# The product with w_in by Strassen's algorithm over halves of 768 tokens, with the weight parts kept in DRAM

## The chip, the core and the metric

The kernel runs on one core of a Trainium2 chip. The metric is the device time of one execution in microseconds. Engines are named as the profile names them: PE is TensorE with its matrix multiplications, PEld its weight loads, DVE is VectorE, ACT is ScalarE, POOL is GpSimd, SP is SyncE, which here only issues DMAs.

## What is computed

```
scores = q @ k.T / 8                     # 8 x 8 heads, 576 positions, head size 64
cum    = cumsum(log(clip(f, 1e-4, 1)))   # decay along the sequence
attn   = softmax(where(causal, scores + cum_i - cum_j, -1e9))
x      = attn @ v                        # laid out as 4608 tokens x 512
h      = x @ w_in                        # w_in: 512 x 2048
g      = h * erf(softplus(h))
out    = g @ w_out                       # w_out: 2048 x 512
```

Everything is float32. w_in and w_out come to the chip as 64-bit numbers, and the kernel makes float32 of them by integer operations (`convert`).

## The kernel before

Each float32 operand of the two large products is held as two float32r parts, a rounded `h` part and the rest `l`, and a product is the sum of h*h, h*l and l*h: three matmuls.

The program has an attention part and then the part called `Moe`. The order of the instructions on PE, ACT, DVE and POOL is the order of the program; the order of the DMAs on SP is chosen when the kernel is built.

**Attention.** A loop over t, 64 + 5 steps, is a pipeline. In step t, PE makes the scores of head half-pair t, the transposes of t-3 (L423) and the products with v of t-4 (L450). DVE adds the decay (L389), ACT takes the exponentials (L401), and POOL normalises t-2 (L411), which the transposes of the next step read. Finished heads go to `xt_d` in DRAM, x transposed. At the end of each step one piece of the weight conversion is run: the first half of the weights, 16 quarters of four pieces each. Quarter u of weight tile a is half of w_in's (i < 2) or of w_out's part (i >= 2). Piece 0 is an Abs on ACT (L293), piece 1 a DVE operation that waits for it (L297), piece 2 two DVE operations (L302, L304), piece 3 a DVE operation (L307), a cast to the h part (L310), the l part on POOL (L311), and the load of the next quarter. The parts stay in SBUF.

**Moe.** Tokens are in chunks of 512, features in groups of 128. A unit is one group of features for one chunk, 144 units in all. The first five chunks are visited for the first eight feature groups, then again for the other eight (their partial sums wait in `part_d`), and the remaining four chunks for all sixteen. For each unit:

- `up` (L135): 4 pieces of the contraction x 3 = 12 matmuls of 512 columns into one PSUM bank of four;
- `softplus` from PSUM (L140) and, for three units together, `erf` (L143), each with its table load on ACT;
- `gate` on DVE (L149, L151) and the l part `gl` on POOL (L152);
- `down` (L171 to L173): 4 token blocks x 3 = 12 matmuls of 512 columns, summed in PSUM over all feature groups of a visit, and at its end copied (L201) or added to the partial sum (L199).

The x of a chunk comes by two DMAs (`xr`) and is split by ACT (L122) and POOL (L123). The first four `up` are run in steps NH to NH+3 of the attention loop, where NH = 64. The second half of the weights is converted in the loop over units, two pieces after each step:

```python
    while moe.more():
        moe.step()
        for _ in range(2):
            if todo:
                convert(*todo.pop(0))
```

## Time and profile before

| | |
|---|---|
| three runs | 1147.81, 1149.36, 1149.46 us; median 1149.36 |
| profiled execution | 1149.86 us, span 1148.1 us, mean granted TensorE clock 0.987 |
| PE busy | 1117.4 us of the span, 7264 matmuls |
| DVE, ACT, POOL busy | 564.8, 624.4, 460.8 us |
| DMA | 120.05 MB, mean 105 GB/s |

Lines of groups read: line of the kernel, engine, operation, what is written from what, shapes and count, then busy time in us and mean ns of one, then the idle time of the engine just before them and what ended it. In lines of a timeline and of the chain in order of time, the first number is the start in us from the start of the span and the second the length. In lines of windows stand the stretch, its length, the busy time of PE, PEld, DVE, ACT and POOL with the number of instructions, the granted clock, the busy share of the DMA engines and GB/s. A busy PE isn't PE at its peak, since the records of matmuls overlap: the pace is read from their starts.

### The profile page before, as it was taken

To read this page: it belongs to the slowest core of one execution; us is meant where nothing else is said; L and a number is where in the kernel's file an instruction comes from. 1 tells how busy PE (TensorE), PEld (TensorE's weight loads), DVE (VectorE), ACT (ScalarE), POOL (GpSimd) and SP (SyncE) were. 2 spreads that over 40 slices of the span, in tenths; PEclk is the share of its full clock that TensorE was granted. 3 is DMA by queue.
4 is the path that set the end of the run, shared out by engine and by line. 5 is a ranking of instruction groups with operands and counts; after the bars stand their busy time and mean duration, and the time that the engine had idled before them with its cause. 6 is when DMAs were issued, how large, how long until landed. Compare 5 with 4: busy or idle time off the path is not lost.

```text
span 1148.1 us, 19397 instructions
## 1 busy us (share of the span) xinstructions
PE 1117.4 (97%) x7264; PEld 923.5 (80%) x7264; DVE 564.8 (49%) x1475; ACT 624.4 (54%) x1251; POOL 460.8 (40%) x532
## 2 busy tenths in 40 slices
PE   5999999999989999999999999999999999999998
PEld 3888888888877878787888888888888888888886
DVE  4788888888855566666322332332322312322221
ACT  3787878787876657557442444343333343344342
POOL 1555556565563444443432432432232232233221
PEclk7999999999999999999999999999999999999999
DMA  7577778778632132230230320320000100000101
GB/s 257 169 249 255 249 231 253 237 245 236 217 118 77 56 113 86 95 109 20 74 106 5 110 98 13 110 92 19 37 19 19 37 19 19 37 19 1 37 1 37
DMA packets 57726, 120.05 MB, mean 105 GB/s; under 512 B 4768, under 2 KB 20128, under 8 KB 57632
## 3 DMA queue, kind: packets, MB, share of 16 engines
q1 hardware_dynamic: 57632, 118.80, 32.0%
q8 instruction: 58, 0.95, 0.3%
q14 instruction: 36, 0.29, 0.1%
HBM read 94.52 MB, written 24.26 MB: 103 GB/s over the span
## 4 chain that ended last, share of the span: by engine, by line
PE 89%; ACT 3%; DVE 2%; DMA 2%; POOL 1%; issue 1%; SPq 0%; ACTq 0%; POOLq 0%; DVEq 0%
PE ph L135 32%; PE y L173 10%; PE y L172 10%; PE y L171 10%; PE s L366 9%; PE o L450 8%; PE t L423 8%; PE s L371 2%; DMA wraw<-in_w_in_dram 1%; POOL xl L123 1%; DMA xr<-xt_d 1%; ACT L143 0%; ACT xh L122 0%; ACT e L143 0%; ACT L293 0%
## 5 line engine op out<-in xcount | busy, mean ns | idle before, releaser
L135 PE MATMUL ph<-xh,w 128*128 128x512 f32 x1152 | 381.7, 392 | 7.3 <-DVE e L149 7.3
L152 POOL TENSOR_TENSOR gl<-e,gh 128x512 fp32r<-128x512 f32 x144 | 186.9, 1299 | 409.0 <-DVE gh L151 392.6
L140 ACT ACTIVATE e<-ph 128x512 f32<-128x512 f32 x144 | 86.1, 598 | 372.9 <-PE ph L135 368.7
L135 PEld LDWEIGHTS ph<-xh,w 128*128 128x128 f32 x1152 | 217.9, 189 | 55.8 <-DVE e L149 7.1
L149 DVE TENSOR_TENSOR e<-e,ph 128x512 f32<-128x512 f32 x144 | 98.1, 681 | 323.6 <-ACT e L143 323.6
L135 PE MATMUL ph<-xl,w 128*128 128x512 f32 x576 | 225.5, 391 | 0.0
L172 PE MATMUL y<-w,gh 128*128 128x512 f32 x576 | 224.1, 389 | 0.0
L173 PE MATMUL y<-w,gl 128*128 128x512 f32 x576 | 224.1, 389 | 0.0
L171 PE MATMUL y<-w,gh 128*128 128x512 f32 x576 | 224.1, 389 | 0.0
L411 POOL TENSOR_SCALAR pr<-pr,st 128x576 f32<-128x576 f32 (+4 forms) x320 | 164.5, 535 | 121.2 <-DVE st L407 94.8
L401 ACT ACTIVATE pr<-pr,st 128x576 f32<-128x576 f32 (+3 forms) x320 | 176.5, 556 | 8.4 <-DVE st L389 8.4
L389 DVE CUSTOM_DVE_ANT_0 pr<-s,c 128x576 f32<-128x576 f32 (+3 forms) x320 | 136.7, 487 | 55.7 <-PE s L371 45.1
L366 PE MATMUL s<-k,q 64*128 64x320 f32 (+4 forms) x768 | 115.3, 426 | 13.4 <-DMA k<-in_k_dram 7.9
L135 PEld LDWEIGHTS ph<-xl,w 128*128 128x128 f32 x576 | 108.8, 189 | 22.3
L172 PEld LDWEIGHTS y<-w,gh 128*128 128x128 f32 x576 | 108.1, 188 | 22.6
L173 PEld LDWEIGHTS y<-w,gl 128*128 128x128 f32 x576 | 108.1, 188 | 22.4
L171 PEld LDWEIGHTS y<-w,gh 128*128 128x128 f32 x576 | 108.0, 188 | 22.4
L151 DVE CAST gh<-e 128x512 fp32r<-128x512 f32 x144 | 92.1, 640 | 61.2 <-PE y L172 46.4
L366 PEld LDWEIGHTS s<-k,q 64*128 64x128 f32 x768 | 75.5, 195 | 43.8 <-issue 19.7
L423 PE MATMUL t<-ident,pr 128*128 128x128 f32 x800 | 104.4, 276 | 4.6 <-ACT pt L432 2.8
L432 ACT COPY pt<-t 128x512 f32<-128x512 f32 x128 | 73.6, 577 | 63.1 <-PE t L423 63.1
L450 PE MATMUL o<-pt,v 128*64 128x128 f32 (+1 forms) x1920 | 103.3, 260 | 0.0
(51 smaller groups left out, 996.3 us busy)
## 6 DMA issues: line engine op xcount, KB each, us to landing
v<-in_vp_dram SPq DMA_DIRECT2D x32, 576.0 KB, 6.4
c<-cum_d SPq DMA_DIRECT2D x62, 288.0 KB, 5.0
xr<-xt_d SPq DMA_DIRECT2D x28, 512.0 KB, 3.5
q<-in_q_dram SPq DMA_DIRECT2D x32, 320.0 KB, 3.6
k<-in_k_dram SPq DMA_DIRECT2D x32, 288.0 KB, 4.2
xt_d<-xo SPq DMA_DIRECT2D x32, 288.0 KB, 5.8
wraw<-in_w_in_dram SPq DMA_DIRECT2D x16, 512.0 KB, 6.0
wraw<-in_w_out_dram SPq DMA_DIRECT2D x16, 512.0 KB, 5.9
```

Source lines behind the costliest of these rows:

```text
L135: nc.tensor.matmul(out=ps, lhsT=w[:, kd, fs], rhs=x[:, kd], start=kd == 0 and n == 0, stop=kd == KD - 1 and n == 2)
L149: nc.vector.tensor_mul(e_, e_, h_)
L152: nc.gpsimd.tensor_tensor(out=gl, in0=e_, in1=gh.bitcast(F32), op=ALU.subtract)
L171: nc.tensor.matmul(out=y[tb], lhsT=gh[:, cs], rhs=wh, start=first, stop=False)
L172: nc.tensor.matmul(out=y[tb], lhsT=gh[:, cs], rhs=wl, start=False, stop=False)
L173: nc.tensor.matmul(out=y[tb], lhsT=gl[:, cs], rhs=wh, start=False, stop=last)
L366: nc.tensor.matmul(out=s[j][:, at:at + k1 - k0], lhsT=q[h, PAD + START[i]:PAD + END[i]], rhs=k[h, k0:k1], start=i > 0, stop=k1 < END[i])
L389: nc.vector.tensor_tensor_reduce(out=to[:, ::-1] if j else to, in0=score, in1=decay_, scale=-0.125, scalar=BIG, op0=ALU.add, op1=ALU.min, ...
L401: nc.scalar.activation(out=seg, in_=seg, func=AF.Exp, bias=st[:, 0, j, m:m + 1], scale=-1.0, accum_out=st[:, 1, j, m:m + 1])
L411: nc.gpsimd.tensor_scalar(out=seg, in0=seg, scalar1=st[:, 2, j, m:m + 1], scalar2=1.0, op0=ALU.mult, op1=ALU.mult)
L423: nc.tensor.transpose(out=b[:, n * P:(n + 1) * P], in_=probs[t][:, at:at + P], identity=ident)
L450: nc.tensor.matmul(out=o[h, to:to + width], lhsT=v[:, ch, h], rhs=pt[:, at[j]:at[j] + width], start=n == 0, stop=n == len(parts) - 1, skip ...
```

## The change

Tokens are now in visits of 768 (two halves of 384), features in groups of 256 (two halves of 128), and a unit is one such group for one visit: 48 units. Three visits take the first four feature groups, then the other four, and the last three visits all eight: nine visits in all. Of each unit:

- `up` makes the four tiles of h (each 128 features x 384 tokens) by Strassen's algorithm in Winograd's form, from seven products over a half of the contraction (2 pieces x 3 matmuls of 384 columns). Products that are only summed share a PSUM bank (`a`, `b`, `x`, `y`, one buffer each). DVE makes the rest of the sums, four operations after the first four products and two after the others. The fifth, sixth and seventh product add to the banks a, x and y, and so follow DVE's reading of these.
- `combine_x` on POOL makes sums of quarters of x, and `split_x` their two parts, for seven matrices of 256 x 384 a visit instead of x itself.
- `activate` takes all four tiles through softplus, then erf. `gate` is one DVE multiplication for each tile; three of the four now read h from SBUF. The rounding to `gh` is now on ACT, `gl` still on POOL.
- `down` has 6 token blocks x 6 matmuls of 512 columns. It sums over the two halves of the unit's features; DVE adds each block (`flush`) to a sum in SBUF, and PSUM has four `y` buffers.
- The order on PE is down(u), up(u+2), down(u+1), and so on.

`convert` now makes for each group the seven sums of parts of w_in and their h and l parts, and the parts of w_out, and writes them to DRAM (`wi_d`, `wo_d`). Each unit loads its own: `load_wi` 1.84 MB, `load_wo` 1.05 MB, two buffers of each. Three calls of two pieces run inside each unit, after the second, fourth and sixth flush. The Abs on ACT is a multiplication on POOL, the h parts are made on ACT. w_in is brought into another order on the host.

```diff
-TB = 512
+TB = 384
+NW = 2 * TB
-HALF = 5
+HALF = 3
+SCRATCH = 1024
...
+    RINGS = {"u": 6, "e": 6, "gh": 6, "gl": 6}
+    PRODUCTS = [("P1", "a"), ("P6", "b"), ("P7", "x"), ("P5", "y"), ("P2", "a"), ("P4", "x"), ("P3", "y")]
+    FIRST = 4
...
+    def combine_x(self, k, part):
...
+        if part == 0:
+            raw[k, "T1"] = self.half("t1", k)
+            sub(raw[k, "T1"], "12", "11")
+            raw[k, "T2"] = self.half("t2", k)
+            sub(raw[k, "T2"], "22", "T1")
+            sub(raw[k, "12"], "22", "12")
+        else:
+            raw[k, "T4"] = self.half("t4", k)
+            sub(raw[k, "T4"], "21", "T2")
+
+    def split_x(self, k, n, vector=False):
...
+        nm = ["11", "T2", "12", "T1", "21", "T4", "22"][n]
...
+        nc.scalar.copy(out=x[:, 0], in_=r)
+        (nc.vector if vector else nc.gpsimd).tensor_tensor(out=x[:, 1], in0=r, in1=x[:, 0].bitcast(F32),
+                                                           op=ALU.subtract)
...
+            for kd in range(2):
+                for i, (w, x) in enumerate(((0, 0), (0, 1), (1, 0))):
+                    nc.tensor.matmul(out=ps, lhsT=wi[:, w, n, kd], rhs=xs[:, x, kd],
+                                     start=not part and kd == 0 and i == 0, stop=kd == 1 and i == 2,
+                                     skip_group_check=True)
...
+        if not part:
+            u2, u3 = self.ring("u", f"2_{u}"), self.ring("u", f"3_{u}")
+            nc.vector.tensor_copy(out=u2, in_=bank["a"])
+            add(u2, bank["b"], u2)
+            add(u3, bank["x"], u2)
+            add(u3, bank["y"], u3)
+            self.h[u] = {"12": u2, "22": u3, "11": bank["a"], "21": self.ring("u", f"1_{u}")}
+        else:
+            h = self.h[u]
+            add(h["21"], bank["x"], h["12"])
+            add(h["12"], bank["y"], h["12"])
...
+    def prepare(self, u):
...
+        if left == 2:
+            self.load_x(k + 1)
+        elif left == 1:
+            self.combine_x(k + 1, 0)
+        elif left == 0:
+            for n in range(3):
+                self.split_x(k + 1, n)
+
+    def prepare_last(self, u):
+        k, a = self.units[u]
+        if a == self.visits[k][1][-1]:
+            self.combine_x(k + 1, 1)
+            for n in range(3, 7):
+                self.split_x(k + 1, n, vector=n % 2 == 0)
+
+    def middle(self, u, tasks):
+        more = u + 1 < self.n
+        self.want_y(u)
+        ys = [self.down(u, tb) for tb in range(NTB)]
+        if more:
+            self.activate(u + 1)
+        order = [("f", 0), ("f", 1), ("g", 0), ("f", 2), ("g", 1), ("f", 3), ("g", 2), ("f", 4), ("g", 3), ("f", 5)]
+        for what, n in order:
+            if what == "f":
+                self.flush(u, n, ys[n])
+                if n in (1, 3, 5):
+                    tasks()
+            elif more:
+                self.gate(u + 1, n)
+        if more:
+            for n in range(4):
+                self.round_gate(u + 1, n)
+        del self.wo[u], self.g[u]
+        self.load_wo(u + 2)
...
     def convert(u, step):
...
-            nc.scalar.activation(out=top, in_=w1_.bitcast(F32), func=AF.Abs)
+            nc.gpsimd.tensor_tensor(out=top, in0=w1_.bitcast(F32), in1=w1_.bitcast(F32), op=ALU.mult)
+            if i == 2:
+                w = sums[a]
+                for out_, in0, in1, op in ((3, 7, 5, ALU.add), (1, 3, 0, ALU.subtract), (2, 0, 7, ALU.subtract),
+                                           (6, 4, 1, ALU.subtract)):
+                    nc.gpsimd.tensor_tensor(out=w[:, out_], in0=w[:, in0], in1=w[:, in1], op=op)
...
+            if i == 2:
+                sums[a, "h"] = hi = cv.tile([P, 7 * 256], F32R, name=f"whi{a}", tag="whi", bufs=1)
+                nc.scalar.copy(out=hi, in_=sums[a][:, :7].rearrange("p i k f -> p (i k f)"))
+                nc.sync.dma_start(out=wi_d[a][:, :7 * 256], in_=hi.bitcast(F32))
...
+            if i == 2:
+                hi, w = sums.pop((a, "h")), sums.pop(a)[:, :7].rearrange("p i k f -> p (i k f)")
+                nc.gpsimd.tensor_tensor(out=w, in0=w, in1=hi.bitcast(F32), op=ALU.subtract)
+                nc.sync.dma_start(out=wi_d[a][:, 7 * 256:], in_=w)
...
-            hi, lo = (moe.w[a][:, 2 * half + i, col] for i in (0, 1))
-            nc.vector.tensor_copy(out=hi, in_=top)
-            nc.gpsimd.tensor_tensor(out=lo, in0=top, in1=hi.bitcast(F32), op=ALU.subtract)
+            hi = cv.tile([P, 7 * 256], F32R, name=f"whi{u}", tag="whi", bufs=1)[:, :DM]
+            nc.scalar.copy(out=hi, in_=top)
+            nc.gpsimd.tensor_tensor(out=top, in0=top, in1=hi.bitcast(F32), op=ALU.subtract)
+            at = (i - 2) * 2 * DM
+            nc.sync.dma_start(out=wo_d[a][:, at:at + DM], in_=hi.bitcast(F32))
+            nc.sync.dma_start(out=wo_d[a][:, at + DM:at + 2 * DM], in_=top)
...
+            if t == NH - 6:
+                moe.load_x(0)
+                moe.load_wi(0)
+                moe.load_wi(1)
+            if t == NH - 5:
+                moe.combine_x(0, 0)
+            if NH - 5 <= t < NH:
+                for n in {1: (0, 1), 2: (2, 3)}.get(t - NH + 6, (t - NH + 7,) if t < NH else ()):
+                    if n == 3:
+                        moe.combine_x(0, 1)
+                    moe.split_x(0, n)
             if NH <= t < NH + 4:
-                moe.step()
+                moe.up((t - NH) // 2, (t - NH) % 2)
+                if t == NH + 1:
+                    moe.load_wi(2)
+                    moe.prepare(1)
+                    moe.activate(0)
+                    for n in range(4):
+                        moe.gate(0, n)
+                        moe.round_gate(0, n)
...
-    w2 = ctx.enter_context(tc.tile_pool(name="w2", bufs=1))
+    moe.wop = ctx.enter_context(tc.tile_pool(name="wop", bufs=1))
+    moe.yp = ctx.enter_context(tc.tile_pool(name="yp", bufs=1))
     moe.ps_y = ctx.enter_context(tc.tile_pool(name="ps_y", bufs=1, space=PSUM))
+    moe.load_wo(0)
+    moe.load_wo(1)
...
+    for u in range(moe.n):
+        moe.middle(u, tasks)
+        if u + 2 < moe.n:
+            moe.prepare(u + 2)
+            moe.up(u + 2, 0)
+            moe.up(u + 2, 1)
+            moe.load_wi(u + 4)
+            moe.prepare_last(u + 2)
```

`wop` and `yp` are opened after the pools of the attention are closed, and their space is taken from it.

More of the change, by code (lines that the diff above doesn't have):

```diff
@@ L152, in gate, with round_gate, down @@
+    def round_gate(self, u, n):
+        c = self.TILES[n]
+        nc = self.nc
+        e_ = self.e[u].pop(c)
+        gh, gl = self.ring("gh", f"{u}_{c}", F32R), self.ring("gl", f"{u}_{c}", F32R)
+        nc.scalar.copy(out=gh, in_=e_)
         nc.gpsimd.tensor_tensor(out=gl, in0=e_, in1=gh.bitcast(F32), op=ALU.subtract)
[L153 to L155 removed]
+        self.g[u][c] = gh, gl
+    def down(self, u, tb):
         nc = self.nc
[L157 to L160 removed]
+        k, a = self.units[u]
+        wo, g = self.wo[u], self.g[u]
+        y = self.ps_y.tile([P, DM], F32, name=f"y{u}_{tb}", tag="y", bufs=4)
+        j, cs = tb // 3, slice(tb % 3 * P, tb % 3 * P + P)
+        for i in range(2):
+            gh, gl = g[f"{i + 1}{j + 1}"]
+            for n, (x, w) in enumerate(((gh, 0), (gh, 1), (gl, 0))):
+                nc.tensor.matmul(out=y, lhsT=x[:, cs], rhs=wo[:, i, w], start=i == 0 and n == 0,
+                                 stop=i == 1 and n == 2)
+        return y
@@ L167, in down @@
-        y = self.y[v]
-        first, last = a == feats[0], a == feats[-1]
-        for tb in range(4):
-            cs = slice(tb * P, tb * P + P)
-            nc.tensor.matmul(out=y[tb], lhsT=gh[:, cs], rhs=wh, start=first, stop=False)
-            nc.tensor.matmul(out=y[tb], lhsT=gh[:, cs], rhs=wl, start=False, stop=False)
-            nc.tensor.matmul(out=y[tb], lhsT=gl[:, cs], rhs=wh, start=False, stop=last)
-            if j == len(self.units) - 1:
-                self.finish_last(y[tb], c * TB + tb * P)
@@ L206, in more @@
-    def more(self):
-        return self.at < self.steps
-    def step(self):
-        j, n = self.at, len(self.units)
-        self.at += 1
-        if j < n:
-            self.up(j)
-            self.want_x(self.units[min(j + 4, n - 1)][0])
-            self.load_x()
-        for i in self.downs[j]:
-            self.down(i)
-        if j in self.ends:
-            for i in self.ends[j]:
-                self.erf(i)
-            self.nc.scalar.preload_act_table_set(SOFTPLUS)
-        if j < n:
-            self.softplus(j)
-        for i in self.gates[j]:
-            self.gate(i)
-        for i in self.downs[j]:
-            self.finish(i)
-        self.split_x()
+                for tb in range(NTB):
+                    self.nc.sync.dma_start(out=self.y[k][tb], in_=self.part_d[v * NTB + tb])
@@ new lines, in flush @@
+    def flush(self, u, tb, y):
+        nc = self.nc
+        k, a = self.units[u]
+        v, feats = self.visits[k]
+        ys = self.y[k][tb]
+        if a:
+            nc.vector.tensor_tensor(out=ys, in0=y, in1=ys, op=ALU.add)
+        else:
+            nc.vector.tensor_copy(out=ys, in_=y)
+        if a == feats[-1]:
+            row = v * NW + tb * P
+            nc.sync.dma_start(out=self.out[row:row + P] if a == NU - 1 else self.part_d[v * NTB + tb], in_=ys)
+    def prepare(self, u):
+        k, a = self.units[u]
+        feats = self.visits[k][1]
+        left = len(feats) - 1 - feats.index(a)
+        if left == 2:
[5 more added lines that the diff above has]
+                self.split_x(k + 1, n)
```

235 lines of the change are left out of this document (109 added, 126 removed).

## The prediction

> **What bounds the kernel now.** I read the page first (engines, slices, chain), then the chain in order of time, the groups by shape, and timelines of single places.
>
> ```profile
> span 1148.1 us, 19397 instructions
> PE   5999999999989999999999999999999999999998
> PE 89%; ACT 3%; DVE 2%; DMA 2%; POOL 1%; issue 1%; SPq 0%; ACTq 0%; POOLq 0%; DVEq 0%
> PE ph L135 32%; PE y L173 10%; PE y L172 10%; PE y L171 10%; PE s L366 9%; PE o L450 8%; PE t L423 8%; PE s L371 2%; DMA wraw<-in_w_in_dram 1%; POOL xl L123 1%; DMA xr<-xt_d 1%; ACT L143 0%; ACT xh L122 0%; ACT e L143 0%; ACT L293 0%
> ```
>
> TensorE carries 89% of the chain. The span is 1148.1 us and this execution took 1149.86, 0.5 us over the median of 1149.36. A time within 0.2% (1147.1 to 1151.7) can't be told from no change. Now the pace of the matrix work:
>
> ```profile
> 639.51 2.72 PE ph L135 x12
> 644.95 2.72 PE ph L135 x12
> 336.08 1.47 PE L423 MATMUL t<-ident,pr 128*128 128x128 f32 x12
> L135 PEld LDWEIGHTS ph<-xh,w 128*128 128x128 f32 x1152 | 217.9, 189 | 55.8 <-DVE e L149 7.1 <-issue 3.1
> L423 PE MATMUL t<-ident,pr 128*128 128x128 f32 x800 | 104.4, 276 | 4.6 <-ACT pt L432 2.8 <-DVE pt L430 1.7
> ```
>
> Two groups of twelve `up` matmuls start 5.44 us apart, with twelve `down` matmuls between: 24 matmuls, 226.7 ns each. The windows show where TensorE isn't full:
>
> ```profile
> 348.00:377.00 29.00, 26.24 (x160) 21.30 (x159) 18.86 (x29) 16.76 (x21) 13.50 (x9) 0.94 0.30 94
> 406.00:435.00 29.00, 27.66 (x121) 22.28 (x120) 20.20 (x27) 20.35 (x24) 13.58 (x10) 1.00 0.36 127
> 464.00:522.00 58.00, 53.92 (x228) 43.55 (x228) 34.65 (x47) 35.49 (x42) 24.14 (x17) 0.97 0.29 99
> 580.00:696.00 116.00, 116.00 (x513) 96.06 (x512) 35.25 (x54) 48.23 (x62) 41.39 (x27) 1.00 0.24 82
> ```
>
> In each row the busy time of PE, PEld, DVE, ACT and POOL follows the length, then the clock. After 580 us nothing is lost. While the second half of the weights is still being converted (to about 520), TensorE is idle for 2.8, 1.3 and 4.1 us in these rows, and 3% less clock in 58 us is another 1.7: 10 us lost in that phase.
>
> **The change: matmuls.** `up` has 1728 matmuls of 512 columns (1152 + 576 of L135). Strassen has 48 units x 7 products x 2 x 3 = 2016 of 384 columns; `down` stays at 1728 of 512. `up` takes 1728 x 226.7 = 391.7 us now. If time goes with columns, a matmul of 384 takes 170.0 ns: 342.7 us, -49.0. If the weight load as recorded, 189 ns, sets the pace, it is 381 us, -10.7. Against that end speaks the row of transposes: (1.47 - 0.276)/11 = 109 ns from start to start, each with a load of 128 f32 columns of its own. A part that doesn't shrink with the columns is likely but no row here gives it; I add 2 ns, 172: 346.8 us, **-44.9**.
>
> A page speaks for more. The Trainium skill, "TensorE: Matmul & The Clock Gate", section "Back-to-back issue gap", gives N/2.4 + 2.5 ns between matmuls; by it 512 columns take 215.8 ns where this trace has 226.7, and 384 would take 162.5, a saving of 64 us. The measurement decides, so the sum doesn't use it.
>
> **A unit after the change, without conversions.** TensorE's unit is 42 x 0.172 + 36 x 0.2267 = 7.2 + 8.2 = 15.4 us. The others:
>
> ```profile
> 318.06 3.65 DMA xr<-xt_d
> L140 ACT ACTIVATE e<-ph 128x512 f32<-128x512 f32 x144 | 86.1, 598 | 372.9 <-PE ph L135 368.7 <-POOL gl L152 3.9
> L143 ACT ACT_TABLE_LOAD x49 | 62.9, 1283 | 0.9
> L152 POOL TENSOR_TENSOR gl<-e,gh 128x512 fp32r<-128x512 f32 x144 | 186.9, 1299 | 409.0 <-DVE gh L151 392.6 <-PE y L172 10.9 <-PE ph L135 5.4
> L123 POOL TENSOR_TENSOR xl<-xr,xh 128x1024 fp32r<-128x1024 f32 x28 | 68.0, 2427 | 84.5 <-ACT xh L122 82.9 <-DVE st L389 1.6
> L122 ACT CAST xh<-xr 128x1024 fp32r<-128x1024 f32 x28 | 29.3, 1045 | 22.1 <-DMA xr<-xt_d 22.0
> L201 DVE COPY yo<-y 128x512 f32<-128x512 f32 x32 | 21.6, 691 | 31.5 <-PE y L173 23.2 <-DMA part_d<-yo 8.4
> L459 DVE COPY xo<-o 128x256 f32<-128x256 f32 x32 | 13.1, 409 | 0.3 <-issue 0.2
> 200.08 0.69 DVE L430 COPY pt<-t 128x512 f32<-128x512 f32 x1
> 200.68 0.68 DVE L297 SCALAR_TENSOR_TENSOR wtop<-wtop,wraw 128x512 f32<-128x512 f32 x1
> 205.75 0.69 DVE L304 SCALAR_TENSOR_TENSOR wraw<-wraw 128x512 int32<-128x512 int32 x1
> L302 DVE TENSOR_SCALAR wraw<-wtop 128x512 int32<-128x512 int32 x32 | 13.8, 433 | 0.0
> ```
>
> DVE: 0.69 us as recorded, but the next starts 0.60 later; for 384 columns, between L459 and L201, 0.55 recorded and 0.47 apart. POOL: 1.30 at 512 and 2.43 at 1024, so 1.02 at 384, 1.86 at 768, 4.1 at 1792. ACT: 0.5 at 384, 0.8 at 768. Per unit ACT has 12 x 0.5 + 2 x 1.28 = 8.6 us, POOL 4 x 1.02 = 4.1, DVE 10 x 0.47 + 6 x 0.60 = 8.3. From the end of `up(u+1)` its last softplus ends at 1.3 us, erfs at 4.6, `gl` at 10.6, and `down(u+1)` starts at 15.4: covered by 4.8. Weights (1.84 and 1.05 MB) have over 20 us to land where 0.5 MB of xr take 3.65 from issue to landing: covered too. SP has little to issue but does it in order: a `load_wi` that waits for `up` holds what stands behind it, part loads and stores, which aren't due before the next `down`. So such a unit costs nothing beside the matmuls; without that cover each us late would cost 48.
>
> **Change of visit.** POOL makes four combinations and five splits, ACT seven copies, DVE two splits. In the unit before, `gl` (to 10.6) is followed by three splits (16.2) and T4 (18.1). ACT's copy of T4 waits for it and its copy of 22 ends at 19.8; DVE's split of that stands ahead of the first flush, which so ends near 22.4. `y` has four banks, so the fifth token block, due at 20.9, waits about 1.6 us. Five visits start outside the conversions: **+8**.
>
> **Conversions among units.** 64 steps remain (16 quarters x 4), at six per unit: 10.7 units. DVE's part of one quarter: 0.60 + (0.34 + 0.61) + 0.60 = 2.15 (L302's 0.43 counts as 0.34, since the next starts 0.09 early), 3.2 per unit. Follow DVE once it is late: after its last conversion one copy (0.65 with the wait) lets the fifth product start, three products (3.1) and two token blocks (2.7) run, and the flush of the second ends 0.9 later: 7.4. Then four flushes, four gates and three calls, 2.4 + 1.9 + 3.2 = 7.5. Sum 14.9, half a us under TensorE's 15.4. Nothing is left for waits. And there are waits:
>
> ```profile
> 414.33 2.84 POOL L123 TENSOR_TENSOR xl<-xr,xh 128x1024 fp32r<-128x1024 f32 x1
> 414.95 2.77 DVE L307 SCALAR_TENSOR_TENSOR wtop<-wtop,wraw 128x512 int32<-128x512 int32 x1
> L304 DVE SCALAR_TENSOR_TENSOR wraw<-wraw 128x512 int32<-128x512 int32 x32 | 38.1, 1192 | 1.1
> DVE wtop L297 <- ACT wtop L293: 41.4, 12, 5.9
> PE ph L135 <- DVE e L149: 7.3, 7, 2.5
> ```
>
> Beside a POOL subtraction the DVE operation on two SBUF tiles took 2.77 us and ended with it, where 0.69 is usual. In a unit 3 gates and 4.5 conversions are of that kind, and four `gl` (1.02 each) run in that stretch. I let two to three of them hold DVE a us each: 2.5 less the 0.5 of room, 2 x 10.7 = +21 (ends: 0 and 4.5 x 10.7 = +48). At three changes of visit the 5 us of late flush find no room: +15. Four times POOL subtracts 1792 columns (4.1) ahead of `lo` and `gl`: 4 x 2 = +8. The 10 us that this phase loses now are replaced: -10. Net **+34**, ends -10 and +65. Abs, its 16 table loads and 32 casts leave ACT and DVE here and in the attention; none ends a wait that I charge.
>
> The Trainium skill, "SBUF — State Buffer", section "Who interferes with whom", states that such a pair of instructions share a port that the first holds to its end. The two timeline rows agree. By that rule alone, with POOL filled to nearly 14 of 15.4 us (`gl` 4.1, visits 9 x 1.86 / 4 = 4.2, quarters 5.6), each of the 7.5 operations would lose about 0.8, some 5.5 per unit and +59; the sum stays with the schedule above.
>
> **Attention, body.** POOL gains per sixteen steps 4 multiplications, 4 sums, one 4.1 us subtraction, and loses two `lo`.
>
> ```profile
> 201.85 2.27 POOL L411 TENSOR_SCALAR pr<-pr,st 128x576 f32<-128x576 f32 x4 [2.95 <-DVE st L407]
> 206.95 2.85 POOL L411 TENSOR_SCALAR pr<-pr,st 128x448 f32<-128x448 f32 x6 [2.83 <-DVE st L407]
> 207.55 1.51 PE L423 MATMUL t<-ident,pr 128*128 128x128 f32 x12
> 360.28 0.39 PE L171 MATMUL y<-w,gh 128*128 128x512 f32 x1
> ```
>
> Normalising ends at 204.12, the transposes that read it start at 207.55: 3.4 us of room, and POOL idles 2.8 to 2.95 a step. Each burst delays it by up to 2.5, so it is hidden; without that cover eight bursts would cost 20. **0**.
>
> **Attention, tail.** From step NH-5 POOL gets 4 + 7 pieces of 1.86 (20.5 us), the sums, a subtraction, `lo` and multiplication of the last quarters (11), and normalising (2.27 or 2.85 a step, 18): 50 us in seven steps of about 5 (206.95 - 201.85). Of the surplus 15 about 3.4 are room. Then `gl` of unit 0 stands on POOL ahead of the last normalising, some 13 us after `up(0)`, with 7 us of work for TensorE meanwhile. Followed step by step, TensorE has its last values at 373 with two units of `up` (14.6 us) done; now its first `down` starts at 360.3 with four of 2.72 done. 373 - 360.3 - 3.7 = **+9** (ends 0, if the room takes it, and +20).
>
> **First weights of `down`.** `wop` takes space that attention used, so `load_wo(0)` waits for it; 1 MB follows, at twice xr's 0.5 MB in 3.65 us some 5.5 with the start. TensorE stands and then has a spell at the lower clock: **+7** (0 if the space is free early, +10 behind the last store). The end has a chain of gates with no `up` over it: +1.
>
> **Sum:** 1149.9 - 44.9 + 8 + 34 + 0 + 9 + 7 + 1 = 1164.0, and 0.5 less as a median: **1164 us** rounded, slower by 1.3%.
>
> **Rivals.** (A) The forecast, DVE tied up in the conversion phase and POOL in the tail: 0.53. (B) Faster: DVE keeps its 14.9 us, since `gl` and the conversions fall apart in time. The phase then costs -10 instead of +34, and the time is 1120. For it: now 41 us of DVE's waits for conversions cost TensorE only 7.3. Against it: DVE was busy 34.65 of 58 us then, 60%, and is to be busy 11.5 of 15.4, 75%, before any wait. It decides when less than about 2 us per unit is lost in all, 21 instead of the 44 that A has. 0.29. (C) `up` gains more than its share of columns: as far under 172 as half the way to the weight load's end, 163.5 ns, saves 17 more: 1147; 0.06. There is one length of this kind in the trace, which can't exclude it. The page's 162.5 ns lies there too. (D) The weight load sets the pace of `up`: 34 us less saved, 1198; 0.05. (E) DVE is held for whole POOL instructions at each meeting: with 4.5 us per unit, 48 instead of 21, and 10 more at the visits, 1201; 0.07. By the page's rule it would be 59.
>
> **The numbers.** Range 1120 to 1200: the low half of B (0.14) and the high half of E (0.04) lie outside. A's own range is 1150 to 1195. Faster takes B and 0.04 of C, 0.33; same takes the rest of C and A's low edge, 0.08; slower 0.59.
>
> **What would show it.** Right: `up` matmuls 172 ns apart; units from the twelfth on 15.4 us apart and, before, 17 to 18; TensorE waiting there for DVE's copy of bank a; in the tail transposes waiting for POOL, then a gap for wo. Wrong: units of 15.4 from the first on (B), or `up` at 160 to 165 (C) or near 190 ns (D). What would upset it most is a load stuck on SP behind one that waits for TensorE, which none of these rows shows.

## The result and the profile after

The changed kernel took 1214.1 us (median of four runs, 1213.35 to 1214.25) beside 1149.4 of the kernel before: ratio 1.0565, 95% interval 1.0546 to 1.0583. The forecast was 1164 with a range to 1200: the direction was right, the size was not, and the time lies above the range. The page after, its span, the slices of PE and of the granted clock, and the shares of the chain:

```profile
span 1212.2 us, 21632 instructions
PE   5999999999885968878779999999999999999998
PEclk7999999999998889888979999999999999999999
PE 57%; POOL 18%; DVE 11%; issue 9%; DMA 3%; ACT 2%; SPq 0%; POOLq 0%; ACTq 0%; DVEq 0%
```

Each slice is 30.3 us. PE's share of the chain fell from 89% to 57%, and PE's gaps lie in the eleventh to twenty-first slice, 303 to 636 us: the end of the attention and the units among which weights are converted. The slices of the attention before that look full, but it was late too. One row of transposes (step 50) before, and then the same step after:

```profile
276.47 1.51 PE L423 MATMUL t<-ident,pr 128*128 128x128 f32 x12
```

```profile
286.61 1.51 PE L510 MATMUL t<-ident,pr 128*128 128x128 f32 x12
```

10.1 us were gone by then. What the change was to bring did come. The chain after 640 us, start and length in us, shows groups of six `up` matmuls:

```profile
646.11 1.06 PE pha L171 x6
647.17 1.04 PE phb L171 x6
648.21 1.04 PE phx L171 x6
```

1.04 / 6 is 173 ns for 384 columns, from start to start over all such pairs 173.4 ns, 1.4 more than forecast: 391.7 - 2016 x 0.1734 = 42 us saved. After 640 us a unit takes 15.51 us from `up` to `up`, except at a change of visit. Before 640 it doesn't. The windows of the changed kernel, with PE's busy time as the second number and the clock behind the five engines:

```profile
396.00:640.00 244.00, 197.55 (x868) 172.89 (x869) 177.27 (x247) 112.31 (x182) 157.88 (x113) 0.89 0.67 238
441.90:444.90 3.00, 0.01 (x1) 0.00 (x0) 0.00 (x0) 0.00 (x0) 3.00 (x2) 1.00 0.76 317
444.90:451.70 6.80, 3.52 (x8) 2.84 (x9) 3.61 (x6) 6.68 (x12) 5.31 (x4) 0.50 0.00 1
```

No engine is busy in more than 81% of those 244 us, and the clock is at 0.89 of full. Rows two and three begin in one wait of PE, from 441.91 to 448.19 us, and show the half clock that set in during the wait and outlasted it. The eleven units of this stretch take 22 us each instead of 15.5.

### The profile page after: what moved, and what is told of

The parts are those of the page before. It is cut to its first block, busy times and chain, and to the rows that moved or that the text cites. A ratio compares the mean times of both kernels' runs of the same rounds, so it can differ in the third digit from the quotient of the medians.

```text
span 1212.2 us, 21632 instructions
## 1 busy us (share of the span) xinstructions
PE 1108.3 (91%) x7552; PEld 966.7 (80%) x7552; DVE 822.8 (68%) x1883; ACT 708.3 (58%) x1532; POOL 659.3 (54%) x691
## 4 chain that ended last, share of the span: by engine, by line
PE 57%; POOL 18%; DVE 11%; issue 9%; DMA 3%; ACT 2%; SPq 0%; POOLq 0%; ACTq 0%; DVEq 0%
PE y L230 20%; PE s L453 7%; PE o L537 6%; PE pha L171 5%; PE phx L171 5%; PE phy L171 5%; PE t L510 5%; POOL gl L218 4%; POOL xs L145 4%; POOL rt L125 3%; DVE ys L250 2%; POOL pr L498 2%; PE phb L171 2%; POOL wa L381 2%; DVE e L210 2%
## 5 line engine op out<-in xcount | busy, mean ns | idle before, releaser
L218 POOL TENSOR_TENSOR gl<-e,gh 128x384 fp32r<-128x384 f32 x192 | 217.2, 1162 | 344.8 <-PE y L230 218.0
L230 PE MATMUL y<-wo,gh 128*128 128x512 f32 x1152 | 361.3, 395 | 30.1 <-DVE ys L250 17.2
L230 PEld LDWEIGHTS y<-wo,gh 128*128 128x128 f32 x1152 | 218.1, 191 | 76.4 <-DVE ys L250 20.2
L230 PE MATMUL y<-wo,gl 128*128 128x512 f32 x576 | 227.4, 395 | 0.0
L250 DVE TENSOR_TENSOR ys<-y,ys 128x512 f32<-128x512 f32 x252 | 172.9, 689 | 78.9 <-PE y L230 76.8
L171 PE MATMUL pha<-xs,wi 128*128 128x384 f32 x576 | 123.6, 351 | 36.4 <-DVE u L181 35.5
L171 PEld LDWEIGHTS pha<-xs,wi 128*128 128x128 f32 x576 | 105.4, 195 | 45.6 <-DVE u L181 30.9
L230 PEld LDWEIGHTS y<-wo,gl 128*128 128x128 f32 x576 | 109.6, 190 | 24.0 <-POOL gl L218 0.7
L171 PE MATMUL phx<-xs,wi 128*128 128x384 f32 x576 | 121.1, 346 | 0.3
L171 PE MATMUL phy<-xs,wi 128*128 128x384 f32 x576 | 118.7, 341 | 0.0
L510 PE MATMUL t<-ident,pr 128*128 128x128 f32 x800 | 106.8, 278 | 10.1 <-POOL pr L498 8.3
```

The source lines that it names most:

```text
L171: nc.tensor.matmul(out=ps, lhsT=wi[:, w, n, kd], rhs=xs[:, x, kd], start=not part and kd == 0 and i == 0, stop=kd == 1 and i == 2, skip_gr ...
L218: nc.gpsimd.tensor_tensor(out=gl, in0=e_, in1=gh.bitcast(F32), op=ALU.subtract)
L230: nc.tensor.matmul(out=y, lhsT=x[:, cs], rhs=wo[:, i, w], start=i == 0 and n == 0, stop=i == 1 and n == 2)
L250: nc.vector.tensor_tensor(out=ys, in0=y, in1=ys, op=ALU.add)
L510: nc.tensor.transpose(out=b[:, n * P:(n + 1) * P], in_=probs[t][:, at:at + P], identity=ident)
```

## The experiments

Lines named L... differ by some between kernels. In each set of up to four kernels the kernel before ran too, at 1146.3 to 1148.0 us. "Excess" is the time from `up` to `up` of successive units, from the third on, less 15.51 us for each.

**e1: no conversions among the units.** The kernel leaves out the second half of the weights, their raw loads and stores included; the loads of wi and of wo read the first four groups' parts throughout.

```diff
-    todo = pieces[2]
+    todo = []
-  in_=self.wi_d[self.units[u][1]])
+  in_=self.wi_d[self.units[u][1] % NU1])
```

> The conversion of the second half of the weights is left out; feature groups 4 to 7 read the parts of groups 0 to 3 from DRAM, so the output differs. Theory (the 71 us by which the eleven units between 396 and 638 us exceed 15.5 each come from the conversions run inside them): those units fall to 15.5 us, three changes of visit keep 2.3 us each, the time is 1214 - 64 = 1150, 1144 to 1156. Rival 1 (the units are slow because the first partial sums, part loads and the clock settle there): at most 15 us go, 1199 or more. Rival 2 (half of it is the change of visit, whose POOL work falls in those units): some 1180.

1153.4 us, ratio 1.0050 (1.0033 to 1.0068). The same stretch:

```profile
395.00:640.00 245.00, 238.63 (x1172) 212.37 (x1173) 149.05 (x248) 138.53 (x231) 138.86 (x96) 0.99 0.64 227
```

The conversions among units cost 61 us. An estimate of how much of it is half clock: here a matmul record is 238.63 / 1172 = 0.2036 us, in the changed kernel 197.55 / 868 = 0.2276. For 868 of them that is some 21 us; the rest was standing still.

**e2: the 128x1792 subtraction on POOL in seven pieces.**

```diff
-  nc.gpsimd.tensor_tensor(out=w, in0=w, in1=hi.bitcast(F32), op=ALU.subtract)
+  for n in range(7):
+      cs = slice(256 * n, 256 * n + 256)
+      nc.gpsimd.tensor_tensor(out=w[:, cs], in0=w[:, cs], in1=hi[:, cs].bitcast(F32), op=ALU.subtract)
```

> The subtraction of 128 x 1792 on POOL (4.0 us, eight times) is cut into seven of 128 x 256. Theory (DVE is held for the whole of that instruction, 4.08 us for an operation of 0.42): DVE gets in between the pieces, the integer operation beside it falls from about 4 to under 1.5 us; in the attention the three steps of delay shrink from 10.1 us to about 5, in the units four times 2 to 3 us go; the seven pieces cost 7 x 0.73 = 5.1 instead of 4.0 us on POOL. Time 1214 - 13 = 1201, 1194 to 1207. Rival (it is the order of POOL's and ACT's work behind the subtraction, not the port): no gain or a us more for each of the eight, 1214 to 1222.

1220.3, ratio 1.0628 (1.0600 to 1.0655). Beside the pieces DVE was no longer held for long: the operation that takes 4.08 us beside the undivided subtraction (its row is shown below, under Conversions) took 0.82 us in e2.

```profile
432.30 0.82 DVE L375 TENSOR_SCALAR wraw<-wtop 128x512 int32<-128x512 int32 x1
```

Yet the excess of the first eleven units behind the first `down` stayed, 69.8 us beside 68.9, and the 6 us were lost ahead of it (402.4 instead of 396.1 us). That isn't proof that such a hold is free: the seven pieces took POOL 5.96 us there instead of 3.99, so e2 trades one for the other. What else costs is seen in the chain of the changed kernel in order of time, through one quarter with the sums:

```profile
419.06 0.70 DVE wa L388
...
419.83 0.75 POOL wa L362
...
420.65 2.96 POOL wa L362 x3
423.63 1.71 ACT whi L370
...
425.40 3.99 POOL wa L381
...
431.91 0.40 POOL wtop L395
...
433.15 3.94 POOL gl L218 x4
```

DVE, POOL, ACT, POOL: each step of the conversion waits for another engine, and `gl`, which PE needs, stands behind them all on POOL.

**e3 and e5: the calls of tasks() moved behind gl.** In e3 all three (one behind the four `round_gate`, two among the pieces of `up`), in e5 the third alone:

```diff
-                if n in (1, 3, 5):
+                if n in (1, 3):
                     tasks()
...
                 self.round_gate(u + 1, n)
+        tasks()
```

> The three calls of conversions in a unit are moved: from behind the second, fourth and sixth flush to behind the rounding of the gates, behind the first four products and behind the other three. Same work. Theory (in the old place they hold the gates, gl and the copy of bank a, which stand behind them on DVE, POOL and ACT): in the new place DVE has 3 us of room before a flush is due, and the 71 us fall to about 35: 1179, 1165 to 1192. Rival 1 (it is the amount of work on DVE and POOL, or weights that land late, not the place): 1205 to 1220. Rival 2 (the activations now stand behind the casts of the conversions on ACT and gl comes late): slower, 1220 to 1240.

> Only the third of a unit's three calls of tasks() moves: from behind the last flush, ahead of the four rounded copies gh and differences gl of the next unit, to behind them. Theory (an in-order queue: the conversion's cast on ScalarE and its differences on GpSimd, 1.7 and 4.0 us in the group with the sums, stand ahead of gh and gl, and the next down product waits for gl): the groups that cost 5.6 to 8 us each because the third call held gl lose most of it, 1185 to 1200 us in all. Rival 1 (the first two calls hold gl just as long, or VectorE's own waits do it): 1208 to 1216. Rival 2 (as when all three calls were moved, 1237: what is put behind gl stands ahead of the next activations and x splits instead): 1218 to 1240.

1237.5 (ratio 1.0774, 1.0753 to 1.0796) and 1238.3 (1.0787, 1.0769 to 1.0806): both slower than the changed kernel. Waits of 396 to 640 us, in all, times and longest, first of the changed kernel, then of e5:

```profile
PE pha L171 <- DVE u L181: 33.7, 10, 6.1
POOL wa L362 <- DVE wa L388: 8.1, 3, 4.5
DVE wtop L366 <- POOL wtop L357: 7.1, 7, 1.6
```

```profile
PE pha L171 <- DVE u L181: 48.5, 10, 11.3
DVE wtop L367 <- POOL wtop L358: 22.0, 9, 5.9
```

A call with steps 0 and 1 holds a POOL product and the DVE step that reads it. By these waits, the product came late when it was put behind `gl`, DVE stood waiting for it, and behind DVE's step stood the copy of bank a for which PE waits. A call can't be moved as a whole.

**e6: steps paired (1,2) and (3,0), raw quarters loaded one further ahead.**

```diff
     todo = pieces[2]
+    convert(*todo.pop(0))
...
-        if u + 1 < 4 * NU:
-            load_weight(u + 1)
+        if u + 2 < 4 * NU:
+            load_weight(u + 2)
```

> Steps of a conversion are paired (1,2) and (3,0 of the next quarter) instead of (0,1) and (2,3), and each raw quarter is loaded one quarter further ahead. So VectorE's step 1 no longer follows the GpSimd product that it reads within one call, and GpSimd's step 0 no longer waits for a load issued just before. Theory (hops between engines inside one call): the waits of VectorE for that product (7.1 us in all), of GpSimd for the raw quarter (8.4 and 3.0 us) go, 1196 to 1207 us. Rival (what holds PE is gl behind the casts and differences, which this leaves where they were): 1210 to 1216.

1227.0, ratio 1.0693 (1.0667 to 1.0719). The waits that it was to remove stayed: from 396 to 640 us POOL waited 14.8 us at once for a raw quarter, where the two such waits of the changed kernel are 8.4 and 3.0, and DVE's waits for the product fell only from 7.1 to 5.6. And the pairing made a hand-over inside a call longer, the sums right behind the DVE step that writes their last input:

```profile
POOL wa L362 <- DVE wa L388: 16.0, 3, 6.4
```

It was 8.1. Theory and rival both missed: they took the old waits as gone and didn't count the one made.

**e7: six visits before the second groups, one step per call.**

```diff
-HALF = 3
+HALF = 6
...
-        for _ in range(2):
-            if todo:
-                convert(*todo.pop(0))
+        if todo:
+            convert(*todo.pop(0))
```

> The first four feature groups are done for all six visits and the last four after them, so the second half of the conversions is spread over 22 units, one step per call instead of two; three more changes of visit (2.3 us each) and twice the partial outputs in DRAM. Theory (a unit has some slack on the in-order engines, and six steps per unit overrun it): the excess of 6.5 us a unit falls to 0 to 1 us, 1160 to 1185 us. Rival (each step costs what it costs, wherever it stands: 61 us for 64 steps): 1214 to 1226.

1192.7, ratio 1.0386 (1.0364 to 1.0409): 21 us better in spite of three more changes of visit. Excess over all units 57 us, where the changed kernel has 80. Between theory and rival: spreading helps, but the order still costs.

**e9: as e7, with the order made for in-order engines.** Place 0 has POOL's product of this quarter, and the sums or the subtraction of what earlier units made; place 1 ACT's casts, of these sums or of what the unit before made; places 2 to 4 a step of DVE each; place 5, behind `gl`, POOL's last difference, SP's stores and the next load.

```diff
+        tasks(u, 0)
         ys = [self.down(u, tb) for tb in range(NTB)]
         if more:
             self.activate(u + 1)
+        tasks(u, 1)
...
                 if n in (1, 3, 5):
-                    tasks()
+                    tasks(u, 2 + n // 2)
...
                 self.round_gate(u + 1, n)
+        tasks(u, 5)
```

> As e7 (six visits of the first four groups, then of the last four), and in the second half of the conversions no engine is handed a step whose input another engine makes in the same call: GpSimd's product, sums or subtraction at the start of a unit, ScalarE's casts behind the activations, VectorE's steps in the three calls, each on what an earlier place or unit made, the last differences and all stores behind gl. One quarter per unit, 16 units. The work is the same. Theory (what costs is in-order engines waiting for each other's conversion steps, and after each wait of PE some us at half clock): of the some 48 us by which e7's units exceed 15.8 us while it converts, the 14 us of the visits stay, 1158 to 1168 us. Rival (VectorE and GpSimd holding each other, or their sheer work, does it): no better than e7, 1188 to 1197.

1180.1, ratio 1.0284 (1.0253 to 1.0316). Excess 44 us, and nearly all of it at changes of visit (two units of 16.9 and 16.4 us behind the conversions, of some 20.2 and 17.8 among them). Units that convert but don't change visit take 15.5. Two and a half of them as a window:

```profile
453.00:492.00 39.00, 39.00 (x193) 34.68 (x192) 30.01 (x49) 23.84 (x40) 26.06 (x18) 1.00 0.89 329
```

PE is never idle, with DVE busy 77% of the time, more than the 73% (177.27 / 244) of the changed kernel's slow stretch, and with a 4.08 us subtraction on POOL at 452.71. So DVE had the time. But e9 moved the meetings of DVE and POOL too: no DVE operation beside that subtraction is longer than usual. Taking the shortest tenth of each kind of DVE operation as usual, the changed kernel's ran some 36 us longer in the 244 us from 396 to 640, e9's some 20 in the 263 us from 397 to 660. e9 also has three buffers for `wtop` and loads raw quarters two ahead; e7 shows no wait for a raw quarter among these units, so the loads aren't the difference, and the buffers weren't tested apart. The theory holds for the units that don't change visit, and the time lies above 1158 to 1168 since I gave the visits 2.3 us each among the conversions too, where they took some 7.

**e14: T4 earlier.** One POOL operation for the next visit's x moved forward:

```diff
             for n in range(3):
                 self.split_x(k + 1, n)
+                if n == 0:
+                    self.combine_x(k + 1, 1)
...
-            self.combine_x(k + 1, 1)
```

> One move: the fourth difference of the next visit's x (T4) is issued on GpSimd right behind the first split of that visit instead of behind the third, one up product later. Theory (ScalarE's rounded copies wait for T4, VectorE's two differences wait for those, and the first flush of the visit and with it the y banks of the down product wait for VectorE): the visits after 640 us lose at least half of their 2.3 us, those among the conversions some 3 us each, 1198 to 1207 us. Rival (VectorE's two differences take the flush's place by their own length, 0.9 to 2.4 us, whenever they can start): 1211 to 1216.

1203.7, ratio 1.0492 (1.0478 to 1.0505). The chain of the changed kernel at a change of visit:

```profile
685.21 2.52 POOL rt L125
...
688.50 0.84 ACT xs L144
...
689.37 0.99 DVE xs L145
690.36 0.61 DVE ys L250
...
691.01 2.35 PE y L230 x9
```

POOL, ACT, DVE, then the flush, then PE. In e14 the chain there is PE alone, with `down` of the new visit in 8.20 us:

```profile
684.29 1.04 PE phy L171 x6
685.33 8.20 PE y L230 x36
693.53 1.06 PE pha L171 x6
```

A visit after 640 us costs 0.1 us instead of 2.3; the excess among the conversions stayed at 69 us.

**e10 and e15: the attention's sums and subtraction in pieces.** In e10 one sum per step, the cast one step behind the last, the subtraction in three. In e15, shown here, the cast comes a step later and the subtraction in two pieces. In both the conversions start one step earlier.

```diff
+        if u < 4 * NU1 and i == 2:
+            add(a, step)
+        if u < 4 * NU1 and i == 3:
+            if step == 1:
+                sums[a, "h"] = hi = cv.tile([P, 7 * 256], F32R, name=f"whi{a}", tag="whi", bufs=1)
+                nc.scalar.copy(out=hi, in_=sums[a][:, :7].rearrange("p i k f -> p (i k f)"))
...
+            elif step:
+                cs = slice(896 * (step - 2), 896 * (step - 1))
+                nc.gpsimd.tensor_tensor(out=w[:, cs], in0=w[:, cs], in1=sums[a, "h"][:, cs].bitcast(F32),
+                                        op=ALU.subtract)
```

> In the attention alone: the four sums go one to a step, the cast of the group one step behind the last, and the subtraction in three pieces over the next three steps (512, 512 and 768 columns); conversions start one step earlier. Theory (the bursts of 4.8 and 4.0 us on GpSimd make the normalisations and so the transposes late, +4.2, +3.4, +2.6 us at three of the groups): the transposes of step 50 come 6 to 10 us earlier than in the changed kernel, 1203 to 1208 us in all. Rival (it is the work, 10 us per group on a GpSimd that the normalisations fill): step 50 within 2 us of the changed kernel, 1211 to 1216.

> As e10, with the group's cast a step later and its subtraction in two pieces over the last two steps, so that the cast does not wait for the store from the one buffer that it shares with the cast of the wo quarter before (1.6 us on ScalarE in e10). Theory (the three losses of the attention body come from a single wait or burst each, in the changed kernel the sums, in e10 that buffer): the transposes of step 50 at 276 to 280 us (before 276.5, changed kernel 286.6), 1203 to 1208 us in all. Rival (it is the amount of work on GpSimd): step 50 at 284 to 287 again, 1210 to 1215.

e10 1212.0, ratio 1.0569 (1.0535 to 1.0602); e15 1205.2, ratio 1.0512 (1.0496 to 1.0529). e10 alone would have shown the work to be the cause: step 50 at 286.1. Its waits from 94 to 106 us show another:

```profile
PE t L528 <- ACT pt L537: 2.4, 1, 2.4
...
ACT whi L362 <- DMA wo_d<-whi: 1.6, 1, 1.6
```

The cast waited for the store from its only buffer, and PE for ACT's copies behind it. With that gone, e15 has step 50 within 0.8 us of the kernel before:

```profile
277.27 1.51 PE L528 MATMUL t<-ident,pr 128*128 128x128 f32 x12
```

**e4 and e8: the first wo load.** e4 allocates `yp` and a tile of 2700 columns ahead of `wop`, which so lies on other space of the attention; e8 gives `xo` a pool of its own that stays, and starts the attention's conversions three steps earlier.

```diff
+    moe.yp.tile([P, PADW], F32, name="pad")
```

```diff
+    xop = ctx.enter_context(tc.tile_pool(name="xop", bufs=2))
-  held["x"] = xo = wk.tile(...)
+  held["x"] = xo = xop.tile(...)
-            if t >= 4 and todo:
+            if t >= 1 and todo:
```

> The pool of the weights of down lies 28 KB higher in each partition, behind yp and a pad, so it no longer covers the tile xo of the last store. Theory (the 12.8 us before the first down are the store of xo, 6.4 us, and then the load of wo, 5.2 us): wo is loaded while the last heads are worked on, the first down follows the last values within 1 us and at the full clock, 1214 - 14 = 1200, 1196 to 1204. Rival (the load waits for the whole pool of the attention, or for its parts to be written): the gap stays, 1212 to 1216.

> The attention's output tiles xo get a pool of their own that stays, so that the first wo load doesn't take over their space, and the conversions in the attention start three steps earlier, so that their last casts and stores don't stand ahead of the last attention outputs. Theory (the 12.8 us before the first down product are the store xt_d<-xo, 6.4 us to landing, behind the two stores of the last quarter on SP): the first down product starts at 384 to 391 us instead of 396, 1202 to 1209 us. Rival 1 (the load is released by something else, or the units with conversions take the lead back): 1211 to 1217, in the first case with the first down product still at 394 to 397.

e4 1217.2, ratio 1.0599 (1.0581 to 1.0616); e8 1209.4, 1.0535 (1.0514 to 1.0556). SP in e4 and in e8:

```profile
382.53 0.32 SPq L398 DMA_DIRECT2D wo_d<-whi  x1
383.88 0.32 SPq L399 DMA_DIRECT2D wo_d<-wtop  x1
384.30 0.57 SPq L553 DMA_DIRECT2D xt_d<-xo  x1
384.92 0.50 SPq L347 DMA_DIRECT2D wraw<-in_w_in_dram  x1
391.00 0.79 SPq L158 DMA_DIRECT2D wo<-wo_d  x2
```

```profile
381.98 0.32 SPq L553 DMA_DIRECT2D xt_d<-xo  x1
382.47 0.80 SPq L157 DMA_DIRECT2D wo<-wo_d  x2
```

In both the load goes behind the last attention output's store, in e4 6.7 us behind (such a store takes a median of 6.4 to land), in e8 0.5, without waiting for the landing. With the other place for `wop` nothing changed, with the other pool for `xo` it did; e15, with the old pool, has the load 8.7 us behind the store (372.58 and 381.25). That fits a release of the attention's pool as a whole. In e4 the store itself stood behind the last conversion's two. e8's 4.7 us can't be given to the load alone: PE's gap before the first `down` fell from 12.8 to 8.4 us, but step 50 came 4.5 us earlier too.

**e11, e13, e17: the end of the attention.** e11 spreads the first visit's x work over steps 45 to 61; e13 puts `normalize` ahead of the first `up` and activations, e17 (shown) `store` too.

```diff
+            if there[2]:
+                normalize(t - 2)
+            if there[5]:
+                store(t - 5)
             if NH <= t < NH + 4:
                 moe.up((t - NH) // 2, (t - NH) % 2)
```

> The loads, differences and splits of the first visit's x are spread over steps 45 to 61 of the attention, one GpSimd operation at a time, instead of the last five steps. Theory (they stand ahead of the last normalisations on GpSimd): the transposes of step 63 start 5 to 12 us earlier, 1202 to 1209 us. Rival (GpSimd has no room earlier either, or the wait for the conversions' stores takes the gain): 1211 to 1218.

> One move: from step 64 of the attention on, the normalisation is issued ahead of the first up products, activations and gates instead of behind them. Theory (the last normalisation stands on GpSimd behind gl of unit 0, which waits for softplus, erf and the rounded copies: 371.5 us instead of some 360): the transposes of step 63 start at 362 to 367 us instead of 374, the first down product at 387 to 391, 1203 to 1209 us. Rival (the stores of the last conversion, which SP issues ahead of the last attention output, hold the first wo load where it is): first down product at 394 to 397, 1211 to 1216.

> As e13, and the copies and the store of the attention outputs are issued ahead of the first up products, activations and gates too. In e13 the normalisation came at 359.6 us, and the transposes of step 63 were as late as before the move, because VectorE's copy of step 62's output stood behind the gates (365.3 us), which wait for the same erf. Theory (the activation of unit 0 stands in the way on GpSimd and on VectorE at once): step 63 at 364 to 368 us instead of 374, first down product at 387 to 391, 1205 to 1210 us. Rival (a third engine holds the same place, ScalarE's copies behind its activations): step 63 at 372 to 375, 1212 to 1216.

e11 1209.6, ratio 1.0531 (1.0494 to 1.0569): step 50 5 us later than in the changed kernel, step 63 4 us earlier. e13 1214.3, ratio 1.0583 (1.0566 to 1.0599): nothing. e17 1207.9, ratio 1.0522 (1.0505 to 1.0540). PE in e13, whose step 63 came at 374.2 as in the changed kernel, and in e17:

```profile
365.85 3.04 PE L537 MATMUL o<-pt,v 128*64 128x128 f32 x32 [4.15 <-DVE xo L546]
```

```profile
368.72 1.67 PE L510 MATMUL t<-ident,pr 128*128 128x128 f32 x13
```

Unit 0's activation stood in two queues at once, on POOL ahead of the normalising and on DVE ahead of the copy of the output. Taking it from one of them brought nothing, from both 5.3 us at step 63.

**e12, e16, e18: together.** e12 is e8, e9, e10 and e11; e16 adds e13 and e14 and has e15 for e10; e18 has e17 for e13 and gives no quarter to the unit behind a visit's x operations:

```diff
+  u, before = (4 * NU1 + 3 * (m // 4) + min(m % 4, 2) if m % 4 != 2 else None for m in (n, n - 1))
```

> e8, e9, e10 and e11 in one kernel. If the four causes are separate and each theory holds: 1192.7 - 28 - 5 - 8 - 8 = 1144 us, taken as 1135 to 1155, about even with the kernel before. If only what e8 and e7 have already shown holds: 1185 to 1192.

> e12 with e13, e14 and e15 in place of e10. If the three theories hold and add up: 1170 - 8 - 20 - 6 = 1136 us, taken as 1130 to 1148, faster than the kernel before. If they do not: 1158 to 1170.

> e16 with e17 in place of e13, and no quarter of a conversion in the unit that follows a visit's last x operations, whose GpSimd starts late (in e16 these units lost 6.2 us each: the sums behind five x operations, the cast behind the sums, gh behind the cast, VectorE's first step behind GpSimd's product). Theory: four to five times 4 to 6 us go there and some 6 at the end of the attention, 1145 - 20 - 6 = 1119 us, taken as 1115 to 1130. Rival (the quarter's wait goes to the next unit): 1138 to 1146.

e12 missed, since e10 and e11 bring little and the visits stayed: 1170.0, ratio 1.0201 (1.0164 to 1.0237); e16 1145.3, 0.9983 (0.9971 to 0.9994); **e18 1134.0, 0.9877 (0.9861 to 0.9894)**: 1.2% less than the kernel before, small but clear of the noise, with the algorithm of the change. POOL in e16 at a visit, which e18 takes apart:

```profile
415.15 4.36 POOL L149 TENSOR_TENSOR xs<-rt,xs 128x768 fp32r<-128x768 f32 x2
419.46 1.04 POOL L682 TENSOR_TENSOR wtop<-wraw 128x512 f32<-128x512 f32 x1
420.46 3.57 POOL L687 TENSOR_TENSOR wa<-wa 128x256 f32<-128x256 f32 x4
426.24 4.62 POOL L222 TENSOR_TENSOR gl<-e,gh 128x384 fp32r<-128x384 f32 x4 [2.21 <-ACT gh L221]
```

In e18 PE's slices are nearly full and the mean granted clock is 0.992, with more work on DVE (75%) and POOL (64%) than in the changed kernel (68% and 54%):

```profile
span 1131.7 us, 21803 instructions
PE   5999999999997899998998999999999999999998
PE 1088.3 (96%) x7552; PEld 951.5 (84%) x7552; DVE 848.2 (75%) x1889; ACT 724.8 (64%) x1553; POOL 722.4 (64%) x722
```

e18 missed 1115 to 1130 by 4 us. Its excess is 24 us, 11 of it in two units of 21 us, and PE still stood 9.8 us before the first `down`. In both units a DVE operation was held by POOL's subtraction. The first of them, POOL and DVE:

```profile
522.41 4.05 POOL L693 TENSOR_TENSOR wa<-wa,whi 128x1792 f32<-128x1792 f32 x1
```

```profile
522.47 4.53 DVE L703 SCALAR_TENSOR_TENSOR wtop<-wtop,wraw 128x512 f32<-128x512 f32 x1
```

In the chain the gates, the flushes and the copy of bank a stand behind it, and then PE. In the other unit it was a gate, 3.75 us from 615.59, beside a subtraction of 4.31. So a hold at the wrong place does cost what the forecast feared.

## Why the prediction was wrong, step by step

Span against span the change cost 1212.2 - 1148.1 = 64 us; the forecast was 14. The step that failed most is the one on conversions among units: it priced DVE held by POOL and had no term for the hand-overs between four in-order queues nor for the half clock, +34 where 59 were measured. Two more failed: the attention's body was put at 0 and cost 10, and the first load of wo at 7 and cost 15. By its terms:

| term | forecast | measured | from |
|---|---|---|---|
| `up` matmuls | -44.9 | -42 | 173.4 ns in the chain |
| five changes of visit | +8 | +11.5 | units of 16.9 and 16.4 us instead of 15.5, five times; e14 takes 10.4 off |
| conversions among units | +34 (44 less 10) | +59 (69 less 10) | excess of the first eleven units; e1 takes 61 off and keeps three visits of 2.3 |
| attention, body | 0 | +10.1 | step 50; e15 gives 9.3 back |
| attention, tail | +9 | +9.1 | last values end 383.2; 383.2 - 10.1 - 360.3 - 3.7 more `up` done |
| first load of wo | +7 | +15 | gap 12.8, then 10.6 us for the first `down`, not 8.2, part of it at half clock |
| end | +1 | about 1 | not measured by itself |

They add to 64. The costs too small are four, the saving too large by 3. The visits went the way that I had followed (e14's chain), at 2.3 us each instead of 1.6. The chain's rows for wo:

```profile
390.89 5.15 issue
396.05 10.56 PE y L230 x36
```

**Conversions.** The place was right, and so was the wait that I had named as a sign: PE's largest one there is for DVE's copy of bank a, 33.7 us. Of the mechanism only a part was right. I had DVE short of time and held by POOL at the shared port. The hold exists. DVE's timeline of the changed kernel, beside the subtraction of 3.99 us at 425.40 (L375 is the L302 of before, there 0.43 us):

```profile
425.60 4.08 DVE L375 TENSOR_SCALAR wraw<-wtop 128x512 int32<-128x512 int32 x1
```

The Trainium skill ("SBUF — State Buffer", "Who interferes with whom") states that lock, and this row agrees with it. It ends 0.3 us after POOL's; the prediction's row of 2.77 us ended 0.55 us after POOL's (417.72 and 417.17), not with it: DVE waited and then ran. The 36 us by which DVE's operations ran longer are 3.3 a unit where I had let 2.5, so the hold's size was near. But only some 7 of the 36 lie on the chain, and shortening the longest holds left the units as they were (e2).

What I had no term for is the hand-over between in-order queues inside one call, which my walk through DVE's queue alone couldn't show: the chain through POOL, ACT and POOL above, calls that cost more when moved as a whole (e3, e5) or paired otherwise (e6), and no cost outside changes of visit once each step stands in a later place than the one that makes its input (e9). How the 59 divide between hand-over and hold stays open, since e9 moved both and e18's two slow units are holds. The half clock, some 21 of the 69, wasn't counted there either. Rival E priced the hold alone and stopped at 1201. The term's ends, -10 and +65, did hold the 59; by its own parts the upper is 48 + 15 + 8 - 10 = 61. One reading was off too: from L302 to the next operation the timeline has 0.45 us (205.30 to 205.75), not 0.34, which leaves 0.3 us of the half a us of room.

**Attention, body.** The 0 named its cover, 3.4 us of room, and the price without it, 20. Three groups took 4.2, 3.3 and 2.6 us instead: not by POOL's amount of work, since e15 does the same, but by sums, cast and subtraction in successive steps, where the room of one step had been counted for each.

**Tail and wo.** That the tail's size came out is luck: I had followed the normalising on POOL alone, and the wait ran through DVE's copy as much (e13, e17). Wo's end of +10, "behind the last store", was the true case, and the store stood behind two others on SP that waited for ACT and POOL. A load "stuck on SP", though behind one that waits for TensorE, I had named as what would upset the forecast most, and gave it no chance of its own. A second sign of it, a raw quarter that was loaded right behind a wi of 1.84 MB and took 10 us to land (572.0 to 582.1), wasn't tested by itself: e6 loads earlier but changes the pairing too.

**Range.** Its upper end came from one term's end (E). Four terms fell to the slow side together. In each of them work was put ahead of other work in a queue that runs in order, which may be why, and I let them stand as independent.

## What to carry to other kernels

Follow a new side task through every queue that it crosses, not only the busiest engine's: hand each engine only what another made one stage earlier, and put POOL's and ACT's parts where that engine waits anyway. e9 did the work that had cost 61 us at no cost but in the units of a visit, where four changes took some 5 us each more than without conversions. Then look where the long instructions of POOL fall beside DVE's: in e9's window the subtraction met nothing that it held, in e18 it held DVE in the two units that took 5.5 us too long. When moving one wait brings nothing (e13, e10), read the new wait before giving up the theory: here a second one of the same length stood behind it.

## What the hardware showed that was not expected

A short stop of PE costs more than its length. In the changed kernel each of the eight stops of 3.28 us or more between 396 and 640 us went with 3.4 or 6.8 us at a granted clock of 0.50, most of it after the stop, and the 12.8 us before the first `down` with 13.7. Below that there is no sharp limit in these traces. In e7, e9 and e16 ten stops behind the first `down` lasted 2.27 to 2.58 us, and six of them had it. In the kernel before a stop of 1.89 us (from 371.3) had it, in e2 one of 3.16 us (from 464.0) had none. The Trainium skill ("TensorE: Matmul & The Clock Gate", "HAM oscillation — how this bites in real kernels") gives stops above about 3.4 us as the limit; by these traces shorter ones can do.

A matmul of this kind costs 173.4 ns for 384 columns and 226.7 for 512. A line through the two has 0.416 ns a column and 13.5 ns that don't shrink; the 2 ns that I had added at 384 columns stand for 8.
